# Four chunks first, casting weight loads, a fixed order on all engines, and crossbar transposes of k, q and x in an attention and feed-forward kernel

## The chip, the cores and the metric

One core of one Trainium2 chip. The metric is the device time of one execution, in microseconds (us); lower is better. Every kernel was checked against the reference, and all the kernels named here gave a correct result. In a run, all kernels and the kernel before take turns on the same chip.

## The reference

Sliding-window attention (8 batches, 8 heads, 576 positions, head width 64, window 64) makes `x` of 4608 tokens by 512; a feed-forward layer with squared ReLU follows.

```python
scores = q @ k^T / sqrt(64), kept only where 0 <= query - key < 64
attn   = softmax(scores);  attn_out = attn @ v
x      = attn_out as [4608, 512]
h      = maximum(x @ w_in, 0.0)          # w_in [512, 2048]
out    = (h * h) @ w_out                 # w_out [2048, 512], float32
```

The kernel works on 36 *chunks* of 128 tokens and nine *blocks* of four chunks (0 to 8).

## The kernel before

While TensorE does the output projection of block g-1 and the up-projection of block g, attention of block g+1 is woven in and block g+2 is loaded. Each chunk is transposed on TensorE: four transposes for k, four for q, and four for the attention result x.

```python
def weave(*streams):                # streams: (steps, lo, hi); steps get even places in lo..hi
    keyed = []
    for s, (steps, lo, hi) in enumerate(streams):
        n = len(steps)
        for i, step in enumerate(steps):
            keyed.append((lo + (hi - lo) * (i + 0.5) / n, s, i, step))
    keyed.sort(key=lambda e: e[:3])
    return [e[3] for e in keyed]

def transposes(i):                  # per chunk, on TensorE
    ps = ps_att.tile([P, 2, HP, P], FP16, name="qkT_ps", tag="ps_a")
    for s, src in enumerate((k16s, q16s)):
        for hp in range(HP):
            nc.tensor.transpose(out=ps[:, s, hp, :], in_=src[i][:, hp * P:(hp + 1) * P],
                                identity=ident[:])
    # ... kT copied out by VectorE, qT by ScalarE

# ... start: chunk 0, all of w_in, chunks 1 to 6 are loaded; chunks 0 to 7 up-projected singly
for s in loads(2):
    s()
for g in range(1, NTB + 1):
    streams = [(ffn_out(g - 1), 0.0, 1.0)]
    if g >= 2 and g < NTB:
        streams.append((ffn_up(g), 0.0, 1.0))
    if g + 1 < NTB:
        streams.append((attention(g + 1), 0.0, 0.95))
    if g + 2 < NTB:
        streams.append((loads(g + 2), 0.0, 1.0))
    for s in weave(*streams):
        s()
```

The kernel is written in this order, but the framework may reorder instructions within an engine. All of block 2 (chunks 8 to 11) is loaded before the loop, and every load and store is issued by SP.

The softmax here doesn't subtract the row's maximum and nothing guards it: scores larger than these inputs give would overflow.

Of the kernel before, what the change touches and what calls it, by code (L numbers as in the profile page):

```python
# [27 lines left out]
def kernel(  # L28
# [17 lines left out]
    W_SCALE = 100.0  # L46
    OUT_SCALE = 1.0 / (W_SCALE * W_SCALE)
# [6 lines left out]
    wst = ctx.enter_context(tc.tile_pool(name="wst", bufs=4))  # L54
    stage = ctx.enter_context(tc.tile_pool(name="stage", bufs=15))
    st16 = ctx.enter_context(tc.tile_pool(name="st16", bufs=8))
    attw = ctx.enter_context(tc.tile_pool(name="attw", bufs=3))
# [8 lines left out]

    ident = const.tile([P, P], FP16, name="ident")
    make_identity(nc, ident[:])





    base = const.tile([P, 64], FP16, name="base")
    nc.gpsimd.memset(base[:], BIG)
    nc.gpsimd.affine_select(
        out=base[:], in_=base[:], compare_op=ALU.is_ge, fill=0.0, base=-1,
        pattern=[[-1, 64]], channel_multiplier=1,
    )
    nc.gpsimd.affine_select(  # L80
        out=base[:], in_=base[:], compare_op=ALU.is_ge, fill=0.0, base=64,
        pattern=[[1, 64]], channel_multiplier=-1,
    )
# [10 lines left out]
    mask_first = make_mask("mask_first", 0)  # L94
    mask_inner = make_mask("mask_inner", None)
    mask_second = make_mask("mask_second", 1)

    w_in_sb = const.tile([P, DMC, DFF], FP16, name="w_in_sb")
    w_out_sb = const.tile([P, FFC, DM], FP16, name="w_out_sb")

    NV = 8
    v_evs = [const.tile([P, H, 66], FP16, name=f"v_ev{i}") for i in range(NV)]
    v_ods = [const.tile([P, H, 66], FP16, name=f"v_od{i}") for i in range(NV)]
    for i in range(NV):
        nc.vector.memset(v_evs[i][:, :, 64:65], 1.0)
        nc.vector.memset(v_ods[i][:, :, 64:65], 1.0)
    nc.vector.memset(v_ods[0][0:64, :, 0:D], 0.0)

    def load_w_in():
        steps = []  # L110
        FQ = DFF // 4

        def one(quar, c):
            ws = wst.tile([P, FQ], FP32, name="ws", tag="ws")
            nc.sync.dma_start(out=ws[:], in_=moe_w_in[c * P:(c + 1) * P,  # L115
                                                      quar * FQ:(quar + 1) * FQ])
            nc.vector.tensor_scalar(  # L117
                out=w_in_sb[:, c, quar * FQ:(quar + 1) * FQ], in0=ws[:],
                scalar1=W_SCALE, scalar2=None, op0=ALU.mult)

        for quar in range(4):
            for c in range(DMC):
                steps.append(lambda quar=quar, c=c: one(quar, c))
        return steps

    def load_w_out():
        def one(f):
            ws = wst.tile([P, DM], FP32, name="ws2", tag="ws")
            nc.sync.dma_start(out=ws[:], in_=moe_w_out[f * P:(f + 1) * P, :])
            nc.gpsimd.tensor_copy(out=w_out_sb[:, f, :], in_=ws[:])  # L130

        return [lambda f=f: one(f) for f in range(FFC)]


    xTs = {}

    def xT_of(g):
        if g not in xTs:
            xTs[g] = xtp.tile([P, DMC, 512], FP16, name="xT", tag="xT")
        return xTs[g]  # L140

    q16s, k16s, qTs, kTs, pms, xs = {}, {}, {}, {}, {}, {}

    def load(i):

        sts = []
        for (src, nm) in ((k, "k"), (q, "q"), (v, "v")):
            st = stage.tile([P, H, D], FP32, name=f"{nm}_st", tag="st")
            b0, j0 = divmod(2 * i, NB)
            if j0 + 1 < NB:  # L150
                nc.sync.dma_start(  # L151
                    out=st[:], in_=src[b0, :, 64 * j0:64 * j0 + P, :].rearrange("h p d -> p h d"))
            else:
                nc.sync.dma_start(
                    out=st[0:64], in_=src[b0, :, 64 * j0:S, :].rearrange("h p d -> p h d"))
                nc.sync.dma_start(
                    out=st[64:P], in_=src[b0 + 1, :, 0:64, :].rearrange("h p d -> p h d"))
            sts.append(st)
        k16s[i] = st16.tile([P, H * D], FP16, name="k16", tag="k16")
        nc.gpsimd.tensor_copy(out=k16s[i][:], in_=sts[0][:].rearrange("p h d -> p (h d)"))  # L160
        q16s[i] = st16.tile([P, H * D], FP16, name="q16", tag="q16")
        nc.gpsimd.tensor_copy(out=q16s[i][:], in_=sts[1][:].rearrange("p h d -> p (h d)"))
        v_ev, v_od, v_next = v_evs[i % NV], v_ods[i % NV], v_ods[(i + 1) % NV]
        nc.gpsimd.tensor_copy(out=v_ev[:, :, 0:D], in_=sts[2][:])
        nc.gpsimd.tensor_copy(out=v_od[64:P, :, 0:D], in_=v_ev[0:64, :, 0:D])
        if i + 1 < NCK:
            nc.gpsimd.tensor_copy(out=v_next[0:64, :, 0:D], in_=v_ev[64:P, :, 0:D])

    def transposes(i):
        ps = ps_att.tile([P, 2, HP, P], FP16, name="qkT_ps", tag="ps_a")  # L170
        for s, src in enumerate((k16s, q16s)):
            for hp in range(HP):
                nc.tensor.transpose(out=ps[:, s, hp, :], in_=src[i][:, hp * P:(hp + 1) * P],  # L173
                                    identity=ident[:])
        kT = attw.tile([P, HP, 192], FP16, name="kT", tag="kT")
        if i > 0:
            nc.vector.tensor_copy(out=kT[:, :, 0:64], in_=kTs[i - 1][:, :, P:192])
        else:
            nc.vector.memset(kT[:, :, 0:64], 0.0)
        nc.vector.tensor_copy(out=kT[:, :, 64:192], in_=ps[:, 0])  # L180
        qT = attw.tile([P, HP, P], FP16, name="qT", tag="qT")
        nc.scalar.activation(out=qT[:], in_=ps[:, 1], func=AF.Copy, scale=1.0)  # L182
        kTs[i], qTs[i] = kT, qT

    def scores(i):
        sc = [ps_att.tile([P, HP, 2, 64], FP32, name=f"sc{hh}", tag="ps_a") for hh in range(2)]
        for hp in range(HP):
            for blk in range(2):
                for hh in range(2):
                    r0 = 64 * hh  # L190
                    nc.tensor.matmul(  # L191
                        sc[hh][:, hp, blk, :], kTs[i][r0:r0 + 64, hp, 64 * blk:64 * blk + P],
                        qTs[i][r0:r0 + 64, hp, 64 * blk:64 * blk + 64], start=True, stop=True)
        j0 = 2 * i % NB
        mask = mask_first if j0 == 0 else mask_second if j0 + 1 == NB else mask_inner
        pms[i] = []
        for hh in range(2):
            pm = attw.tile([P, HP, 2, 64], FP16, name=f"pm{hh}", tag=f"pm{hh}")
            nc.scalar.activation(out=pm[:], in_=sc[hh][:], func=AF.Exp,
                                 scale=1.0 / float(D) ** 0.5)  # L200
            nc.vector.tensor_tensor(out=pm[:], in0=pm[:], in1=mask, op=ALU.min)
            pms[i].append(pm)

    def values(i):
        x_sb = attw.tile([P, H, D], FP16, name="x_sb", tag="x_sb")
        for half in range(2):
            av = ps_att.tile([P, 4, 66], FP32, name="av", tag="ps_a")
            for h in range(4 * half, 4 * half + 4):
# [8 lines left out]
                out=x_sb[:, 4 * half:4 * half + 4, :], in0=av[:, :, 0:D],  # L217
                in1=rden[:].to_broadcast([P, 4, D]), op=ALU.mult)
        xs[i] = x_sb

    def to_xT(i):
        xt = ps_att.tile([P, DMC, P], FP16, name="xt_ps", tag="ps_a")
        for c in range(DMC):
            nc.tensor.transpose(out=xt[:, c, :], in_=xs[i][:, 2 * c:2 * c + 2, :],  # L224
                                identity=ident[:])
        nc.vector.tensor_copy(out=xT_of(i // 4)[:, :, (i % 4) * P:(i % 4 + 1) * P], in_=xt[:])  # L226

    def attention(g):

        steps = []  # L230
# [7 lines left out]
    def loads(g):  # L238
        return [lambda i=i: load(i) for i in range(4 * g, 4 * g + 4)]


    h2s = {}

    def ffn_up(g):
        h2s[g] = h2pool.tile([P, FFC, 512], FP16, name="h2", tag="h2")

        def one(f):
            hps = ps_up.tile([P, 512], FP32, name="hps", tag="ps_u")
            for c in range(DMC):
                nc.tensor.matmul(  # L250
                    hps[:], w_in_sb[:, c, f * P:(f + 1) * P], xT_of(g)[:, c, :],
                    start=(c == 0), stop=(c == DMC - 1))
            hrelu = hrp.tile([P, 512], FP32, name="hrelu", tag="hrelu")
            nc.scalar.activation(out=hrelu[:], in_=hps[:], func=AF.Relu)  # L254
            nc.vector.scalar_tensor_tensor(  # L255
                out=h2s[g][:, f, :], in0=hps[:], scalar=0.0, in1=hrelu[:],
                op0=ALU.max, op1=ALU.mult)

# [53 lines left out]
    for s in load_w_in():  # L312
        s()
# [55 lines left out]
```

## Time and profile before

The median is 348.6 us (347.5 to 349.0).

| | before |
|---|---|
| span of the profiled run | 345.9 us |
| TensorE (PE) busy | 324.3 us, 94% |
| first up-projection / first output store | 19.4 us / 78.7 us |
| a steady block, from its first output projection to the next block's (130.4 to 266.5 us) | 34.0 us |

The page's busy shares, and its time line in 40 slices (each digit tenths of a slice; PEclk is TensorE's granted clock in tenths). PE is TensorE, PEld its weight loads, DVE is VectorE, ACT ScalarE, POOL GpSimd and SP the sync engine; SPq marks a DMA that SP issues, with the time that the issue alone took:

```profile
PE 324.3 (94%) x3146; PEld 178.2 (52%) x3146; DVE 207.9 (60%) x506; ACT 163.8 (47%) x289; POOL 121.5 (35%) x204
...
PE   1957888999999999999999999999999999999995
...
PEclk9996999999999999999999999999999999999998
DMA  7799987899972455546877757730011000000021
```

After the ninth slice (about 75 us) TensorE has no gap until the end: there only TensorE work can be saved. The chain that ended last, inside a block (start us, us, what):

```profile
109.11 0.86 PE ops L296 x4
...
110.62 0.22 PE qkT_ps L173 x4
...
122.10 0.22 PE xt_ps L224 x4
```

Four 512-wide matmuls take 0.86 us and four transposes 0.22 us. A block has 48 transposes, thus 12 x 0.22 = 2.6 us. The time line of TensorE has the first up-projection:

```profile
121.90 0.36 SPq L303 DMA_DIRECT2D out_dram<-osb  x1
122.35 0.39 SPq L151 DMA_DIRECT2D k_st<-in_k_dram  x1
```

```profile
19.41 1.05 PE L271 MATMUL hps_446<-xT,w_in_sb 128*128 128x128 f16 x16 [0.98 <-DVE xT L226]
```

### The profile page before, as it was taken

The page shows a single profiled execution, that of the slowest core. Times are in us where ns is not written, and L with a number is a line of the kernel's source. Part 1 is how long each engine was busy: PE and PEld are TensorE (multiplying, and loading weights), DVE is VectorE, ACT ScalarE, POOL GpSimd, SP SyncE. Part 2 cuts the span into 40 slices and gives each one's busy share as a digit, 9 for nine tenths or more (in the row PEclk, how much of TensorE's full clock was granted, in tenths as well). Part 3 has the DMA queues.
Part 4 walks back from the last instruction along what each step waited for, and adds up shares of the span by engine and source line. Part 5 has one row for each costly group of instructions (what it writes and reads, how often), then busy time and mean ns, then how long its engine had stood idle before and what let it go on. Part 6 is the DMA issues. An engine that isn't in the chain of part 4 may idle for free.

```text
span 345.9 us, 7917 instructions
## 1 busy us (share of the span) xinstructions
PE 324.3 (94%) x3146; PEld 178.2 (52%) x3146; DVE 207.9 (60%) x506; ACT 163.8 (47%) x289; POOL 121.5 (35%) x204
## 2 busy tenths in 40 slices
PE   1957888999999999999999999999999999999995
PEld 0346787875555555445545554455445544544442
DVE  2656988852666776676776657665675566544400
ACT  1123457544535646643664466436544654444411
POOL 4009895497753333316566544530000000000000
PEclk9996999999999999999999999999999999999998
DMA  7799987899972455546877757730011000000021
GB/s 200 249 252 239 234 247 252 207 230 228 243 172 61 93 121 123 121 124 155 212 185 182 170 135 184 185 87 27 23 45 36 30 32 32 30 30 32 35 88 62
DMA packets 122341, 46.65 MB, mean 135 GB/s; under 512 B 113600, under 2 KB 113600, under 8 KB 122304
## 3 DMA queue, kind: packets, MB, share of 16 engines
q1 hardware_dynamic: 122304, 46.15, 51.7%
q8 instruction: 24, 0.39, 0.5%
q14 instruction: 13, 0.11, 0.1%
HBM read 36.70 MB, written 9.44 MB: 133 GB/s over the span
## 4 chain that ended last, share of the span: by engine, by line
PE 83%; DVE 7%; DMA 5%; ACT 2%; SPq 1%; issue 1%; ACTq 0%
PE ops L296 37%; PE hps L250 28%; DMA ws<-in_moe_w_in_dram 5%; PE qkT_ps L173 4%; PE av L211 4%; PE xt_ps L224 2%; DVE h_397 L276 1%; DVE h_1087 L276 1%; DVE xT L226 1%; DVE w_in_sb L117 1%; PE hps_639 L271 1%; SPq L151 1%; SPq L115 0%; PE hps_1088 L271 0%; PE hps_1537 L271 0%
## 5 line engine op out<-in xcount | busy, mean ns | idle before, releaser
L250 PE MATMUL hps<-xT,w_in_sb 128*128 128x512 f16 x448 | 115.2, 379 | 0.0
L254 ACT ACTIVATE hrelu<-hps 128x512 f32<-128x512 f32 x112 | 66.8, 598 | 91.6 <-PE hps L250 90.9
L250 PEld LDWEIGHTS <-w_in_sb 128*128 128x128 f16 x448 | 43.7, 98 | 52.6 <-issue 0.3
L271 PEld LDWEIGHTS <-w_in_sb 128*128 128x128 f16 x512 | 31.2, 99 | 8.2 <-issue 3.9
L301 ACT ACTIVATE osb<-ops 128x512 f32<-128x512 f32 x36 | 21.6, 600 | 29.1 <-PE ops L296 28.9
L182 ACT ACTIVATE qT<-qkT_ps 128x512 f16<-128x512 f16 x36 | 21.5, 596 | 22.6 <-DVE kT L180 22.3
L216 DVE TENSOR_TENSOR x_sb<-av,rden 128x256 f16<-128x256 f32 x72 | 27.5, 415 | 0.1
L180 DVE COPY kT<-qkT_ps 128x512 f16<-128x512 f16 x36 | 15.2, 421 | 18.0 <-PE qkT_ps L173 17.8
L226 DVE COPY xT<-xt_ps 128x512 f16<-128x512 f16 x36 | 15.1, 420 | 12.7 <-PE xt_ps L224 12.7
L215 DVE RECIPROCAL rden<-av 128x4 f32<-128x4 f32 x72 | 11.4, 178 | 17.1 <-PE av L211 17.1
L255 DVE SCALAR_TENSOR_TENSOR h_5222<-hps,hrelu 128x512 f16<-128x512 f32 x16 | 11.1, 691 | 16.6 <-ACT hrelu L254 16.6
L296 PE MATMUL ops<-w_out_sb,h_1087 128*128 128x512 f16 x64 | 17.5, 380 | 0.0
L191 PEld LDWEIGHTS <-kT 64*128 64x128 f16 x576 | 11.0, 95 | 12.2 <-issue 9.6
L296 PE MATMUL ops<-w_out_sb,h_3120 128*128 128x512 f16 x64 | 16.5, 380 | 0.0
L296 PE MATMUL ops<-w_out_sb,h_2579 128*128 128x512 f16 x64 | 16.5, 380 | 0.0
L296 PE MATMUL ops<-w_out_sb,h_4199 128*128 128x512 f16 x64 | 16.5, 380 | 0.0
L296 PE MATMUL ops<-w_out_sb,h_3658 128*128 128x512 f16 x64 | 16.5, 380 | 0.0
L296 PE MATMUL ops<-w_out_sb,h_2041 128*128 128x512 f16 x64 | 16.5, 380 | 0.0
L296 PE MATMUL ops<-w_out_sb,h_4736 128*128 128x512 f16 x64 | 16.4, 379 | 0.0
L296 PE MATMUL ops<-w_out_sb,h_397 128*128 128x512 f16 x64 | 15.3, 380 | 0.0
L224 PE MATMUL xt_ps<-ident,x_sb 128*128 128x128 f16 x144 | 15.1, 222 | 0.1
L255 DVE SCALAR_TENSOR_TENSOR h_4736<-hps,hrelu 128x512 f16<-128x512 f32 x16 | 11.0, 689 | 6.8 <-ACT hrelu L254 6.4
(837 smaller groups left out, 611.1 us busy)
## 6 DMA issues: line engine op xcount, KB each, us to landing
out_dram<-osb SPq DMA_DIRECT2D x36, 256.0 KB, 2.2
k_st<-in_k_dram SPq DMA_DIRECT2D x32, 256.0 KB, 3.9
q_st<-in_q_dram SPq DMA_DIRECT2D x32, 256.0 KB, 4.0
v_st<-in_v_dram SPq DMA_DIRECT2D x32, 256.0 KB, 4.1
ws<-in_moe_w_in_dram SPq DMA_DIRECT2D x16, 256.0 KB, 4.2
k_st<-in_k_dram SPq DMA_DIRECT2D x8, 128.0 KB, 3.2
q_st<-in_q_dram SPq DMA_DIRECT2D x8, 128.0 KB, 3.0
v_st<-in_v_dram SPq DMA_DIRECT2D x8, 128.0 KB, 3.2
```

Source lines behind the costliest of these rows:

```text
L173: nc.tensor.transpose(out=ps[:, s, hp, :], in_=src[i][:, hp * P:(hp + 1) * P], identity=ident[:])
L180: nc.vector.tensor_copy(out=kT[:, :, 64:192], in_=ps[:, 0])
L182: nc.scalar.activation(out=qT[:], in_=ps[:, 1], func=AF.Copy, scale=1.0)
L216: nc.vector.tensor_tensor(out=x_sb[:, 4 * half:4 * half + 4, :], in0=av[:, :, 0:D], in1=rden[:].to_broadcast([P, 4, D]), op=ALU.mult)
L224: nc.tensor.transpose(out=xt[:, c, :], in_=xs[i][:, 2 * c:2 * c + 2, :], identity=ident[:])
L226: nc.vector.tensor_copy(out=xT_of(i // 4)[:, :, (i % 4) * P:(i % 4 + 1) * P], in_=xt[:])
L250: nc.tensor.matmul(hps[:], w_in_sb[:, c, f * P:(f + 1) * P], xT_of(g)[:, c, :], start=(c == 0), stop=(c == DMC - 1))
L254: nc.scalar.activation(out=hrelu[:], in_=hps[:], func=AF.Relu)
L255: nc.vector.scalar_tensor_tensor(out=h2s[g][:, f, :], in0=hps[:], scalar=0.0, in1=hrelu[:], op0=ALU.max, op1=ALU.mult)
L271: nc.tensor.matmul(hps[:, f, :], w_in_sb[:, c, (4 * fq + f) * P:(4 * fq + f + 1) * P], xT_of(g)[:, c, t0:t0 + P], start=(c == 0), stop=(c ...
L296: nc.tensor.matmul(hold["ps"][:], h2s[g][:, f, ts * P:(ts + 1) * P], w_out_sb[:, f, :], start=(f == 0), stop=(f == FFC - 1))
L301: nc.scalar.activation(out=osb[:], in_=hold["ps"][:], func=AF.Copy, scale=OUT_SCALE)
```

## The change

The intent: shorten the start (four chunks before any weights, weights cast by the DMA itself, a weight quarter used for four chunks), fix the order of all engines as written, and from block 3 on take all transposes off TensorE by letting the DMA crossbar do them (a DMA within SBUF, the on-chip memory, that transposes on its way). The diff, cut to its core:

```diff
-    nc.sync.dma_start(out=ws[:], in_=moe_w_in[...])             # and a cast by DVE or POOL
+    def load_w_in(quar):
+        nc.gpsimd.dma_start(out=w_in_q[quar][:], in_=moe_w_in[...])   # fp32 in, fp16 out
 ...
+    def transposes_xbar(g):                        # four chunks of k, then of q
+        for key, dst in (("k", kT_of(g)), ("q", qT_of(g))):
+            nc.sync.dma_start_transpose(
+                out=dst[:].rearrange("p a (c t) -> p (a c) t", t=P),
+                in_=kqs[key, g][:].rearrange("p a c t -> p (a c t)"))
+        nc.vector.tensor_copy(out=kBs["b", g][:, :, 64:P], in_=kTs["k", g][:, :, 0:64])
 ...
+    def to_xT_xbar(i):                             # two chunks of x
+        nc.sync.dma_start_transpose(out=xT_of(i // 4)[...], in_=xs[i // 2][...])
 ...
+    ctx.enter_context(tc.manual_schedule(engines={E.PE, E.Activation, E.DVE, E.Pool, E.SP}))
 ...    # start: chunks 0 to 3, w_in, chunks 4 to 7, w_out, chunks 8 and 9
+        if g >= XBAR_FROM:                         # XBAR_FROM = 3
+            steps = [lambda: transposes_xbar(g), lambda: scores(4 * g)]
+            for i in range(4 * g, 4 * g + 4):
+                def step(i=i):
+                    values(i)
+                    if i % 4 < 3:
+                        scores(i + 1)
+                    if i % 2:
+                        to_xT_xbar(i)
+                steps.append(step)
+            return steps
 ...
-    for s in loads(2):
-        s()
     for g in range(1, NTB + 1):
+        # out_proj(g-1) 0..1 and up(g) 0..1 as before
+        if g == 1:
+            streams.append((loads(2, 2) + loads(3), 0.0, 1.0))   # chunks 10, 11, 12 to 15
         if g + 1 < NTB:
-            streams.append((attention(g + 1), 0.0, 0.95))
+            streams.append((attention(g + 1), 0.0, 0.9))
-        if g + 2 < NTB:
+        if g >= 2 and g + 2 < NTB:
             streams.append((loads(g + 2), 0.0, 1.0))
```

By `weave`, a block's events stand at these places (fractions of the block): k and q transposes 0.075, first scores 0.225, x transposes 0.525 and 0.825.

## The prediction

> **What bounds the kernel now.** Three stretches of the trace:
>
> (a) 0 to 75 us, start and first eight chunks. The chain of waits begins with four waits for first-layer weights (5.5, 4.3, 3.8, 5.4 us); the first up-projection ends about 26.5 us after the start; the output projection leads the chain only from 75.4 us. The stretch table shows the DMA engines 76 to 104% busy from 10 to 60 us: k, q and v come in 256-byte packets (113600 of 122341 packets are under 512 B) at 200 to 260 GB/s. TensorE is 57 to 91% busy there. DMA and long dependency chains bound it.
>
> (b) 99 to 300 us, six pipelined blocks of about 33.5 us. TensorE is always busy and the chain lies nearly wholly on it: four 512-wide matmuls take 0.86 us, 128 of them 27.6 us; scores and values about 0.38 us per chunk each (3 us per block); the 48 transposes 0.22 us per four, 2.7 us per block. Sum 33.3 us. DVE (22 of 34 us), ACT (18), POOL and DMA have room.
>
> (c) 300 to 346 us: the last 192 matmuls of 512 columns and the last store. Untouched.
>
> **What the change does.**
> 1. Start: four chunks go through attention first; their k and q come in four-row (1 KB) runs; the DMA casts the weights, so 16 DVE and 16 POOL casts go; a weight quarter serves several chunks before the next is needed. Estimate from the rates above: chunks 0 to 3 (3 MB) land by about 12 us, the first weight quarter by 17 instead of 25. Then 32 chunk-quarters at 1.05 us (33.6 us), the remaining attention (about 8 us) and some waits: output projection from about 63 us instead of 75. Gain 12 us; DMA needs about 55 us for what is required by then, so hardly more.
> 2. Blocks 3 to 8: 48 TensorE transposes per block go, with 8 PSUM copies on DVE (0.42 us each) and 4 on ACT (0.6 us). On the critical path: 6 x 2.7 = 16 us.
> 3. Added: per block two 512 KB and two 256 KB crossbar transposes on SP's queue. The Trainium skill, "DMA: Bandwidth & Descriptors", section "Latency and other measured facts", gives 261 GB/s for a DMA transpose; no run here shows it yet. Estimate with that: 2 us for k, 2 for q, 1 per x, plus about 2 us landing (stores here land in 2.2 us): 6 us of DMA time per block. Bandwidth is there (40 to 80% busy). Latency is the risk: k and q are issued just before block start, DVE stands in line behind k (the boundary copy), and the first scores come about 7 us into the block. I allow up to 2 us of new TensorE waits per block, 5 us in all.
>
> **Sum.** 348.6 - 12 - 16 + 5 = 325 us (rounded). Range 313 to 338. Faster by over 2%: 0.93; within 2%: 0.05; slower: 0.02.
>
> **What would show it.** Block period falls from 33.5 to about 31 us from block 3; TensorE transposes of k, q, x remain for twelve chunks; TensorE busy falls by about 20 us; long runs of output projections start near 63 us; crossbar transposes land in 3 to 6 us; waits of scores for q stay under 2 us each.
>
> **What would make it wrong.** Crossbar transposes much slower than ordinary DMAs (over 8 us for k plus q): then DVE waits for k, TensorE for PSUM and scores, and the 2.7 us per block is given back. SP blocked by long transpose issues, so that loads come late. POOL's descriptor work for casting loads delaying the k and v casts at the start, eating the 12 us.

## The result, and the profile after

The change is slower: 358.7 us median (356.9 to 360.6) against 348.8 of the kernel before in the same rounds. Ratio 1.030, 95% interval 1.025 to 1.035. All outputs are right. Ratios here are the mean time of one kernel's fast runs over that of the other's in the same rounds, so they are not quite the ratio of the medians. Where I turn a difference of ratios into time I multiply by 348 us.

The page of the kernel after, the same rows:

```profile
PE 311.8 (87%) x2855; PEld 163.8 (46%) x2855; DVE 183.3 (51%) x427; ACT 155.3 (44%) x270; POOL 115.4 (32%) x191
...
PE   4878788794995999799979989995999899999995
...
PEclk9989999997896999999999999999699999999999
DMA  7999999018599667965995599649935922210021
```

TensorE is busy 12.5 us less (324.3 to 311.8), but its idle time, span less busy, grew from 21.6 to 44.5 us. There are holes at every block's start, and the DMA row reads 0 and 1 in slices 8 and 9: for about 16 us, from 62 us on, almost nothing was moved, while loads were still due.

**The first hole.** The SP time line and the TensorE time line:

```profile
53.32 6.12 SPq L100 DMA_DIRECT2D st<-in_v_dram  x1
78.16 0.36 SPq L307 DMA_DIRECT2D out_dram<-osb  x1
78.61 0.39 SPq L100 DMA_DIRECT2D st<-in_k_dram  x1
```

```profile
23.28 1.89 PE L283 MATMUL hps<-xT,w_in 128*128 128x128 f16 x16 [0.46 <-DMA w_in<-in_moe_w_in_dram]
...
84.04 0.40 PE L180 MATMUL qkT_ps<-ident,k 128*128 128x128 f16 x4 [4.00 <-POOL k L117]
...
111.33 1.01 PE L272 MATMUL hps<-xT,w_in 128*128 128x512 f16 x2 [5.20 <-DVE h L266]
```

SP issued its last load of the start at 53 us and the next one only at 78.6 us, right after the first output store. The loads of the next chunks stand behind that store in SP's order, and the store waits for TensorE. At 84 us TensorE has just waited 4.0 us for the k cast of such a late chunk, and before 111 us it waited 5.2 us, because VectorE, which had to empty the PSUM buffer (PSUM is the memory that TensorE writes to), was itself waiting for k. The chain of waits there:

```profile
105.93 4.50 DMA kT<-k
110.43 0.02 issue
110.45 0.23 DVE kB L197
110.68 0.61 DVE h L266
111.29 0.04 issue
111.33 1.86 PE hps L272 x4
```

TensorE's first line above also shows that the up-projection starts at 23.3 us, later than before (19.4). The first output store comes 0.5 us earlier (78.16 against 78.67), and the output projection, which led the chain from 75.4 us before, starts at 72.4 us: of the 12 us expected, the start gained 0.5 to 3.

**The blocks.** Who waited for whom (total us, times, longest us):

```profile
DVE kB L197 <- DMA kT<-k: 26.3, 6, 7.1
...
PE hps L272 <- DVE h L266: 16.2, 6, 5.2
```

The boundary copy of k (kB: the last 64 keys of the block before and the first 64 of this one, side by side, which the first scores read) waits 26.3 us in six blocks, 4.4 us each; TensorE then waits 16.2 us for VectorE. But the crossbar is no slower than predicted. The DMA issues, with the median time from issue to landing:

```profile
xT<-x_sb SPq DMA_TRANSPOSE x12, 3.1
kT<-k SPq DMA_TRANSPOSE x6, 4.5
qT<-q SPq DMA_TRANSPOSE x6, 4.4
```

What is late is the issue. SP's time line at the start of a block:

```profile
130.59 0.36 SPq L307 DMA_DIRECT2D out_dram<-osb  x1
135.00 1.24 SPq L254 DMA_TRANSPOSE xT<-x_sb  x1
136.29 0.57 SPq L100 DMA_DIRECT2D st<-in_k_dram  x1
136.91 0.65 SPq L100 DMA_DIRECT2D st<-in_q_dram  x1
137.61 0.90 SPq L100 DMA_DIRECT2D st<-in_v_dram  x1
138.61 0.97 SPq L307 DMA_DIRECT2D out_dram<-osb  x1
140.59 2.61 SPq L194 DMA_TRANSPOSE kT<-k  x1
143.29 2.01 SPq L194 DMA_TRANSPOSE qT<-q  x1
```

From 131 to 135 us SP stands at the x transpose, whose data VectorE writes. Only then does it issue the loads of the block's fourth chunk. The k transpose needs that very chunk, since it takes four chunks at once; it waits for the load and its cast, is issued 2.6 us into the block (the block's first output projection starts at 138.0 us), and k lands at 140.6 + 4.5 = 145.1 us, when TensorE and VectorE are well into the block. In the kernel before, each chunk was transposed by itself, in mid-block, so a late fourth chunk hurt nobody (e3 below has the same late loads, and its blocks take 34.0 us as before). The Trainium skill, "DMA: Bandwidth & Descriptors", section "Anatomy of one DMA — SWDGE (gpsimd) path", states that DMA engines never wait on semaphores and that any such wait happens on the issuing sequencer before dispatch. The section is about DMAs that GpSimd issues, but its sentence is general, and these lines of SP agree: the queue behind the waiting transpose stood for 4 us.

### The profile page after: what moved, and what is told of

Same layout as the page of the kernel before. It is cut to its first block, busy times and chain, and to the rows that moved or that the text cites. A ratio compares the mean times of both kernels' runs of the same rounds, so it can differ in the third digit from the quotient of the medians.

```text
span 356.3 us, 7207 instructions
## 1 busy us (share of the span) xinstructions
PE 311.8 (87%) x2855; PEld 163.8 (46%) x2855; DVE 183.3 (51%) x427; ACT 155.3 (44%) x270; POOL 115.4 (32%) x191
## 4 chain that ended last, share of the span: by engine, by line
PE 55%; DMA 22%; DVE 7%; ACT 5%; SPq 5%; POOL 4%; issue 2%; POOLq 0%; ACTq 0%
PE ops L300 24%; PE hps L272 20%; DMA st<-in_v_dram 10%; PE hps L283 5%; DMA qT<-q 5%; DVE h L266 4%; SPq L100 4%; ACT hrelu L265 3%; DMA kT<-k 3%; PE sc L209 3%; PE av L233 3%; DMA w_in<-in_moe_w_in_dram 2%; POOL v_ev L123 1%; DMA st<-in_q_dram 1%; DVE x_sb L238 1%
## 5 line engine op out<-in xcount | busy, mean ns | idle before, releaser
L266 DVE SCALAR_TENSOR_TENSOR h<-hps,hrelu 128x512 f16<-128x512 f32 x144 | 98.8, 690 | 102.2 <-ACT hrelu L265 101.1
L300 PE MATMUL ops<-w_out,h 128*128 128x512 f16 x576 | 149.1, 387 | 0.0
L272 PE MATMUL hps<-xT,w_in 128*128 128x512 f16 x448 | 117.4, 385 | 16.2 <-DVE h L266 16.2
L300 PEld LDWEIGHTS <-h 128*128 128x128 f16 x576 | 53.7, 99 | 61.2 <-issue 3.3
L272 PEld LDWEIGHTS <-w_in 128*128 128x128 f16 x448 | 44.3, 99 | 71.5 <-issue 20.4
L218 ACT ACTIVATE pm<-sc 128x512 f16<-128x512 f32 x72 | 39.1, 596 | 8.0 <-PE sc L209 6.0
L283 PE MATMUL hps<-xT,w_in 128*128 128x128 f16 x512 | 33.5, 223 | 4.9 <-DVE h L266 4.4
L283 PEld LDWEIGHTS <-w_in 128*128 128x128 f16 x512 | 30.7, 100 | 6.1 <-issue 4.9
L123 POOL CAST v_ev<-st 128x512 f16<-128x512 f32 x36 | 22.8, 634 | 24.6 <-DMA st<-in_v_dram 23.1
L222 DVE TENSOR_TENSOR pm<-pm,mask_inner 128x512 f16<-128x512 f16 x56 | 26.3, 492 | 7.9 <-ACT pm L218 7.3
L124 POOL COPY v_od<-v_ev 64x512 f16<-64x512 f16 x36 | 22.3, 619 | 2.3
L126 POOL COPY v_od<-v_ev 64x512 f16<-64x512 f16 x35 | 21.6, 617 | 2.0
L233 PEld LDWEIGHTS <-pm 128*64 128x64 f16 x576 | 12.5, 112 | 14.7 <-DVE h L266 7.6
```

The costliest lines, as they stand in the source:

```text
L123: nc.gpsimd.tensor_copy(out=v_ev[:, :, 0:D], in_=st[:])
L218: nc.scalar.activation(out=pm[:], in_=sc[hh][:], func=AF.Exp, scale=1.0 / float(D) ** 0.5)
L222: nc.vector.tensor_tensor(out=pm[:], in0=pm[:], in1=mask, op=ALU.min)
L233: nc.tensor.matmul(av[64 * blk:64 * blk + 64, h % 4, 0:65], pms[i][h % 2][:, h // 2, blk, :], vv[:, h, 0:65], start=True, stop=True)
L266: nc.vector.scalar_tensor_tensor(out=out, in0=hps, scalar=0.0, in1=hrelu, op0=ALU.max, op1=ALU.mult)
L272: nc.tensor.matmul(hps[:], w_in_q[f // 4][:, c, f % 4 * P:(f % 4 + 1) * P], xT_of(g)[:, :, c, :], start=(c == 0), stop=(c == DMC - 1))
```

## The experiments

Theory A: loads stand in SP's fixed order behind instructions that wait for compute, come late, and the four-chunk transposes turn late loads into waits. Rival B: the crossbar transposes themselves (4.5 us to land, and their load on the DMA engines) cost the time. Rival C: the start and the fixed order cost it whatever transposes. All the experiments start from the kernel after. One caution: e1 scatters (343.4 to 350.2 us), and two of its four runs, the profiled one among them, are slow and left out of the ratio. The ratio thus rests on two runs, and I do not read e1 closer than its interval.

**e1: chunks 10 and 11 ahead of the first store**

```diff
+    load_chunk(10)
+    load_chunk(11)
     U(7, 0), U(7, 1), U(7, 2), U(7, 3)
 ...
-            streams.append((loads(2, 2) + loads(3), 0.0, 1.0))
+            streams.append((loads(3), 0.0, 1.0))
```

> Only the loads of chunks 10 and 11 move ahead of the first output projection in SP's program order; nothing else changes. Theory A (loads stand in SP's fixed order behind instructions that wait for compute, so they come late; the crossbar itself is fast enough): the idle DMA stretch 62 to 78 us goes, TensorE's 4 to 6 us hole at 80 us goes, and the first k transpose is issued several us earlier; time falls by 6 to 12 us, to 347 to 352 us. Later blocks keep their waits of about 4 us for k. Rival B (the transposes' own latency of 4.5 us and their load on the DMA engines cost the time): the hole at 80 us goes, but at most 5 us is won, 354 us or more.

348.8 us, ratio 0.993 (0.984 to 1.002), against 1.030 of the change: about 13 us won by the ratios, 10 by the medians, and DVE's six waits for k are still 24.3 us. The order of two chunks' loads alone takes back the loss, as far as the interval tells.

**e2: all later loads in the first 0.6 of their block**

```diff
-            streams.append((loads(3), 0.0, 1.0))
+            streams.append((loads(3), 0.0, 0.6))
-            streams.append((loads(g + 2), 0.0, 1.0))
+            streams.append((loads(g + 2), 0.0, 0.6))
```

> As e1, and all later loads are placed in the first 0.6 of their block, so that the fourth chunk's loads are issued before the second x transpose. Theory A: the k transpose is issued right after the block's last output store instead of after a late cast; DVE's wait for k falls from 26 us in six waits to under 10, and the time to about 330 us (325 to 338). Rival B: DVE still waits about 4 us for each k, blocks stay at 33 us or more, time 345 or more.

330.4 us, ratio 0.949 (0.946 to 0.953). This is the change with nothing but its loads moved, 28 us faster than it (348 x (1.030 - 0.949)). DVE's waits for k fell to 11.1 us, a little more than the 10 expected:

```profile
DVE kB L197 <- DMA kT<-k: 11.1, 6, 3.2
```

Two successive k transposes are issued at 125.22 and 156.65 us: a block takes 31.4 us, as predicted for the change itself. By the start of each block's output projection, 8 of the 28 us lie in the block that waited for chunks 10 and 11 (27.5 us in the change, 19.8 here) and the other 20 in the six blocks with crossbar transposes (33.7 to 38.1 us in the change, 31.3 to 33.1 here). Rival B forecast 345 or more and is out as the main cause.

**e3: no crossbar, loads left late**

```diff
-    XBAR_FROM = 3
+    XBAR_FROM = 99
```

> All transposes back on TensorE, loads where the change has them. Theory A: transposes by chunk need the fourth chunk's load only in mid-block, so the blocks lose little: block period 33.5 us again, the hole at 80 us stays; 345 to 352 us, faster than the change though TensorE has 16 us more to do. Rival C (the start and the fixed order cost the time, not the transposes): 360 us or more, since the 16 us of TensorE work come on top.

349.9 us, ratio 1.004 (1.002 to 1.007). With late loads, taking the crossbar away *helps* by 9 us, although TensorE gets its transposes back. Rival C forecast 360 or more.

**e4: SP's order left to the framework**

```diff
-    ... engines={E.PE, E.Activation, E.DVE, E.Pool, E.SP}))
+    ... engines={E.PE, E.Activation, E.DVE, E.Pool}))
```

> SP is taken out of the engines whose program order is fixed, all else as in the change. Theory A: loads may then move ahead of stores and transposes that wait; time falls by 10 us or more, to 335 to 348 us. If the order on SP comes out the same, the time stays at 358 and the run tells nothing. Rival B: within 4 us of the change whatever the order.

335.4 us, ratio 0.963 (0.960 to 0.966). The instruction order of the four other engines is identical to the change's; only SP's order differs. Its time line shows loads for later chunks issued straight through from 62 to 81 us, and no wait of VectorE for k is left. So 23 us of the change's time hang on SP's order alone.

**e5: early loads, no crossbar**

```diff
 # e2, and
-    XBAR_FROM = 3
+    XBAR_FROM = 99
```

> The loads of e2 (early) with every transpose on TensorE. With e2 at 330.4 this prices the crossbar transposes by themselves once loads are in time. If their worth is TensorE's time alone, 16 us: 346 us, so only 4 us better than e3 and still about level with before. If early loads are worth as much here as they were to the change (28 us): 322 us, and the crossbar would cost time even then. Expected: 342 to 346.

344.1 us, ratio 0.990 (0.986 to 0.994). With e2, e3 and the change this makes a square of four medians:

| | loads late | loads early |
|---|---|---|
| transposes on TensorE | 349.9 (e3) | 344.1 (e5) |
| crossbar from block 3 | 358.7 (change) | 330.4 (e2) |

The crossbar costs 9 us when loads are late and wins 14 us when they are in time. The early loads are worth 6 us without (5 by the ratios) and 28 us with the crossbar. It is the combination that fails.

**e10 and e11: the fourth load moved**

```diff
 # e1, and in the blocks
-            streams.append((loads(g + 2), 0.0, 1.0))
+            streams.append((loads(g + 2), 0.0, 0.92))    # e10: fourth load at 0.805
+            streams.append((loads(g + 2), 0.0, 0.8))     # e11: fourth load at 0.70
```

> e1 with one more shift: in the blocks the fourth chunk's load goes from 0.875 to 0.805 of the block, just ahead of the second x transpose (0.825) but still behind the third output store (0.72). If standing behind the x transpose makes the load late, k is issued 2 to 3 us earlier per block and the time falls from e1's 348.8 to 333 to 340. If standing behind the store is enough to make it late, the time stays at 345 to 349.

> As e10, the fourth load at 0.70 of the block, ahead of the third store too. If the x transpose was the obstacle, nothing more than e10 (within 2 us). If the store was, this is where the gain comes: 332 to 337, near e2's 330.4.

A comparison of e10's instruction order with e1's shows a single kind of change: on SP, in five blocks, the three loads of the fourth chunk and the second x transpose change places. (POOL's order is the same; on VectorE and ScalarE only buffer numbers differ.) e10 runs in 332.4 us, ratio 0.954 (0.949 to 0.959), 14 us less than e1 by the ratios (16 by the medians). In e11 the fourth load goes ahead of the store too, and the third, at 0.5, comes ahead of the first x transpose (0.525), which the expectation does not mention: 330.7 us, ratio 0.952 (0.948 to 0.957), no clear further gain. So standing behind the waiting x transpose was what mattered; standing behind the store was not. SP's time line in e10 at the same point of a block, and the wait that answers to it:

```profile
120.67 0.43 SPq L100 DMA_DIRECT2D st<-in_k_dram  x1
121.15 0.71 SPq L100 DMA_DIRECT2D st<-in_q_dram  x1
121.90 0.96 SPq L100 DMA_DIRECT2D st<-in_v_dram  x1
124.67 1.73 SPq L254 DMA_TRANSPOSE xT<-x_sb  x1
127.65 0.36 SPq L307 DMA_DIRECT2D out_dram<-osb  x1
128.11 2.08 SPq L194 DMA_TRANSPOSE kT<-k  x1
```

```profile
DVE kB L197 <- DMA kT<-k: 10.9, 6, 4.5
```

The loads now use the time in which SP would have stood. From the x transpose to the k transpose it takes 3.4 us (124.67 to 128.11) against 5.6 us in the change (135.00 to 140.59), k is issued 0.4 us into the block and not 2.6, and VectorE's waits for k fall to 10.9 us, from 26.3 in the change (24.3 in e1, whose profiled run is slow).

**e6, e12, e15: crossbar for k and q only**

```diff
 # e6: the change's late loads
-                    if i % 2:
-                        to_xT_xbar(i)
+                    if i % 4:
+                        to_xT(i - 1)             # on TensorE; the last one a step of its own
 # e12: e2's early loads; values, scores and to_xT as 13 single steps
 # e15: as e12, but
+                streams.append((steps[:2], 0.0, 0.3))     # k and q at 0.075, first scores at 0.225
+                streams.append((steps[2:], 0.3, 0.9))
```

> The change's own late loads, crossbar for k and q only; x goes back to TensorE, so SP no longer stands at an x transpose before the block's last load. Theory A in detail (the x transpose at 0.825 of a block is what holds back the load at 0.875, hence the cast, hence k): DVE's waits for k fall from 4.4 us each to under 3, and the time to 340 to 350 us although TensorE gets 5 us more work. If the stores alone hold the loads back, the waits stay and the time is about 363.

> e2's early loads, crossbar for k and q, x on TensorE with its steps woven singly (e6 gave each x transpose to one step together with scores and values, five PSUM buffers in a ring of four, and its chain shows waits for that). x on TensorE costs 0.9 us in six blocks: 335 to 338. If k and q by crossbar are in themselves bad, as e6's 378 might say, it stays above 344.1 (e5).

> e12 with the k and q transposes and the first scores put back to 0.075 and 0.225 of the block, as in e2; in e12 the greater number of steps had moved the scores to 0.10, about 3 us after the block's start, while q lands about 7 us after it. If that distance is what made e12 slow (373), this runs in 334 to 339. If the x transposes on TensorE or k and q by crossbar without x are to blame, it stays above 350.

e6 ran in 378.2 us (ratio 1.087) and e12 in 373.1 us (ratio 1.073): both missed widely, against theory A as I had written it. VectorE's waits for k did fall in e6 (16.6 us), but the scores now waited for q, which e12 shows too:

```profile
PE sc L209 <- DMA qT<-q: 27.0, 6, 6.1
```

The fault was in my edits: more steps in the same stretch moved the first scores from 0.225 to 0.19 (e6) and 0.10 (e12) of the block. In e12's chain of waits k is issued at 132.0 us and q lands at 138.9: q comes 7 us after k's issue, and a place 3 us after the block's start is too early. e6 in addition asked five PSUM buffers of a ring of four per chunk. In e15, with the scores back at 0.225, the time is 342.6 us (ratio 0.984), 30 us less than e12, and the same wait is down to 2.9 us. That settles the greater part: the distance between issue and first use (e15 also places the steps after the first scores later, at 0.3 to 0.9). e15 is still 4 us above the top of what I expected; its chain shows TensorE waiting for x and the mask on VectorE in mid-block, and I did not take that apart. Against e5, with every transpose on TensorE, it is 2 us better by the ratios with overlapping intervals: that the crossbar pays for k and q alone is not shown.

**e7: crossbar for x only, loads late**

```diff
-        if g >= XBAR_FROM:                               # the k and q steps
+        if False:
 ...
+        # per-chunk transposes as in blocks 0 to 2, but to_xT_xbar for x from block 3
```

> The change's own late loads, crossbar for x only; k and q chunk by chunk on TensorE. Theory A: nothing at a block's start needs the last chunk of the block, so late loads do no harm after the first block; against e3 (349.9) TensorE saves 0.9 us per block: 343 to 348 us, no wait of DVE over 2 us in the blocks. Rival B (any crossbar traffic slows the blocks): 352 or more.

344.2 us, ratio 0.989 (0.987 to 0.992): 5.2 us better than e3 by the ratios, where TensorE saves 6 x 0.9 = 5.4 us. x by crossbar gives its full worth even with late loads, because nothing at a block's start needs the block's last chunk.

**e8: four PSUM buffers at the start**

```diff
 # e2, and for the up-projections of chunks 0 to 7
-        hps = ps_up.tile([P, 4, P], FP32, name="hps4", tag="ps_u")
+        pool, tag = ((ps_up, "ps_u"), (ps_out, "ps_o"))[turn[0] % 2]
+        turn[0] += 1
+        hps = pool.tile([P, 4, P], FP32, name="hps4", tag=tag)
```

> e2, with the up-projections of the first eight chunks taking four PSUM buffers in turn in place of two (the output projection's two are idle then). The start gave 3 us where 12 were predicted; if the loop matmul, ACT, DVE over two buffers sets the pace there (two groups per 2.47 us in the trace, where TensorE needs 2.1), the output projection starts 4 to 8 us earlier and the time falls to 323 to 327. If the arrival of weights and chunks sets it, the time stays at 330.

326.0 us, ratio 0.937 (0.931 to 0.943), 4 us less than e2. The first output store, in e2 and in e8:

```profile
77.91 0.36 SPq L307 DMA_DIRECT2D out_dram<-osb  x1
```

```profile
72.80 0.36 SPq L311 DMA_DIRECT2D out_dram<-osb  x1
```

So part of the start is the round trip matmul, ScalarE, VectorE over two buffers, as expected.

**e16: the first weight quarter first**

```diff
 # e8, and
+    load_w_in(0)                      # at the head of POOL's work
     for i in range(NV):
         nc.vector.memset(v_evs[i][:, :, 64:65], 1.0)
 ...
-    for quar in range(3):
+    for quar in range(1, 3):
         load_w_in(quar)
```

> e8 with the first weight quarter's load moved to the head of POOL's work, ahead of the casts of chunks 1 to 3. The prediction had this quarter landing at 17 us; it landed at 23. If its late issue (15.7 us) sets the start, the first up-projection and the first output store come 3 to 6 us earlier and the time is 320 to 323. If the DMA engines, full from the start, set it, the chunks come later by what the weights gain: 325 to 328.

329.5 us, ratio 0.947 (0.943 to 0.951), 3 us *slower* than e8 (0.931 to 0.943; the intervals just touch). The first up-projection moves from 22.9 to 27.2 us. The weight quarter now lands at 10.6 us in place of 22.8, but the loads beside it land later: the first half of chunk 1's k at 12.1 us in place of 7.8. What one transfer gains, others lose; in the first 60 us of the change the DMA engines' mean busy share reads 1.09. Chunk 0's q had landed by 5.6 us in both runs, yet ScalarE cast it at 12.8 us in place of 8.4. ScalarE issues the q loads of the first chunks, and its sixth load, which stands before that cast, was held until just that half of chunk 1's k had landed, though the program has no such dependence. So this too is an engine held at a DMA issue with work behind it, and the run does not tell the load on the DMA engines from the order of the queues.

**e13 and e14: an attempt to beat both**

```diff
 # both: e8, and k and q issued at 0.94 of the block before
+        if XBAR_FROM <= g + 2 < NTB:
+            streams.append(([lambda g=g: transposes_xbar(g + 2)], 0.9, 0.98))
 # e13: boundary copy of k right before the first scores (0.225)
 # e14: boundary copy at 0.075
```

> A version meant to beat both kernels: e8 (early loads, four PSUM buffers at the start), k and q transposes issued at 0.94 of the block before, and the boundary copy of k moved behind them to just before the first scores, so that DVE does not stand in line. Theory A: the remaining waits at a block's start go (0.4 us in each block and 2 us at 95 us): 321 to 325, with DVE's waits for k under 3 us in all.

> e13 missed: there the boundary copy of k stood right before the first scores and TensorE waited for DVE to reach it (1.9 us per block). Here k and q are issued at 0.94 of the block before, as in e13, but the boundary copy stands at 0.075, so both k has landed when DVE gets there and the copy is done when scores need it. Theory A: no wait for k or q over 0.5 us in the blocks; 321 to 325 against e8's 326. If issuing k and q ahead of the last store costs as much as it wins, 326 to 330.

e13 missed: 331.4 us, ratio 0.955. VectorE no longer waits for k to land, but it reaches the boundary copy only after its other work, and TensorE waits for it:

```profile
PEld L208 <- DVE kB L387: 13.2, 6, 2.6
```

e14 puts the copy at a place where k has landed and the scores are not yet due: 323.4 us (322.1 to 324.9), ratio 0.930 (0.925 to 0.935). One wait for k is left, in the first crossbar block:

```profile
DVE kB L199 <- DMA kT<-k: 3.9, 1, 3.9
```

e14 beats the kernel before by 7%, the change by about 10% (0.930 / 1.030 = 0.903, an estimate over two sets of rounds). Against e8 the gain is 2.6 us by the ratios, and the two intervals overlap, so that last step is likely but not shown.

## Why the prediction was wrong

- **Step 3, the waits ("up to 2 us of new TensorE waits per block, 5 us in all").** This is the step that failed. VectorE waited 4.4 us per block for k and TensorE's idle time grew by 22.9 us. I had judged the crossbar's landing time, and that was right (medians of 3.1 to 4.5 us, inside my 3 to 6; one k took 6.1). I had assumed that "k and q are issued just before block start". They were issued 2.6 us into the block or later (0.4 to 0.6 us in e2 and e10, from the second crossbar block on), because SP, in fixed order, stood at the second x transpose with the fourth chunk's load behind it. Swapping just these two in five blocks gave about 14 us (e10 against e1). Of my warnings, "SP blocked by long transpose issues, so that loads come late" came nearest, but SP was held by a wait for data, not by the length of the issue.
- **Left out altogether: the loads of chunks 10 and 11.** The change moves them from before the loop to behind the first output store. I read the diff for what is added and removed and did not follow SP's order. DMA stood idle from 62 to 78 us, TensorE waited 4.0 and 5.2 us, and e1 won 10 to 13 us by moving them back.
- **Step 1, the start (12 us expected; 0.5 us measured by the first output store, 3 us by the start of the output projection).** Mis-sized from a misreading: I took "the first weight quarter" of the kernel before to land at 25 us. That is the last of its 16 weight loads (25.1 us); the first four had landed by 10.2 us, and the first up-projection starts at 19.4 us. In the change the first quarter lands at 23.2 us, later than before, and the first up-projection starts at 23.3 us. Two PSUM buffers set part of the pace after that (e8: 5.1 us on the first store). The start and the fixed order of the engines were not tested apart; together, with loads in time and no crossbar, they are worth 3.6 us (e5, ratio 0.990). What else kept the start from the 12 us stays open.
- **Step 2, the transposes (16 us).** Right in kind. In kernels whose loads come in time, k, q and x by crossbar are worth 14 us (e5 to e2) after their own waits, where the prediction's 16 less 5 makes 11. TensorE's busy time fell 12.5 us in the change where I had said 20; it fell 21.7 us in e2 (324.3 to 302.6). That the waits themselves lengthen busy time is seen below.
- **The sum.** With its loads in time the change runs in 330.4 us (e2), inside the range that I gave for the change itself. What was predicted was a kernel whose queue order works. That even this lands in the range owes something to its width: the start's term was about 8 us too large (e5: 3.6 us in place of 12).

One further cost: the Trainium skill, "TensorE: Matmul & The Clock Gate", Part 1, states that the array clock falls to half after an idle window of about 3.4 us. The trace agrees: after the 5.2 us hole before 111.3 us the chain shown above has four matmuls of 512 columns at 1.86 us instead of 0.86, matmuls at half speed also follow the holes of 4.0 us (before 84.0) and 3.9 us (before 249.4), and the page's PEclk reads 6 to 8 around them. The four holes of 1.6 to 1.9 us at the other blocks' starts are followed by matmuls at full speed (0.215 us each). A long hole thus costs more than its length.

## What to carry to other kernels

On an engine that issues DMAs in a fixed order, every instruction that waits for compute holds up all the loads behind it; so write out the order of that one queue and ask of each load what it stands behind and who needs it next. Crossbar transposes save TensorE work, but batching them over four chunks moves the deadline of the last chunk's load from mid-block to block start, so the loads have to move with it. When a step is taken off an engine, keep the distance between its issue and its first use longer than its landing time (here 7 us for k and q together), and check that nothing in order behind it stands in line.

## What the Trainium skill lacked or had wrong

- "DMA: Bandwidth & Descriptors", section "Latency and other measured facts", gives 261 GB/s for a DMA transpose, measured on one kernel with a non-contiguous middle dimension, but no time to landing for a single one. From SBUF to SBUF here, 256 KB land in 3.1 us and 512 KB in 4.5 us, thus 0.524 MB / 4.5 us = 116 GB/s to landing. The difference of the two sizes, 0.262 MB in 1.4 us, makes 187 GB/s as an estimate, beside other traffic. This does not show the page's figure wrong: with 2 us for landing added, the prediction drew 4 us for k from it, and 4.5 were measured.
- The same page, section "Issuing engines are not separate DMA queues", calls the sequencer's issue time usually small relative to the DMA. Here issuing one crossbar transpose of 512 KB kept SP for 2.0 to 3.5 us of the 4.4 to 6.1 us to its landing, and issuing a single 256 KB load took 6.1 of 11.8 us (the line at 53.32) while the DMA engines were full.
- That the wait stands on the issuing sequencer is in the skill, as cited above. No page that I read gives a measured case of what such a wait costs a kernel through the loads queued behind it; here it was worth 23 us (e4, where SP's order alone differs).
